# A transformer-like block in split fp32: the second product of an MLP unit accumulates in PSUM onto a ScalarE copy of the first

## The chip, the cores and the metric

The kernel runs on one core of a Trainium2 chip. The metric is the device time of one execution in microseconds (us). The core's engines run side by side, each through its own queue in order: TensorE (PE in the profile, with PEld for its weight loads), VectorE (DVE), ScalarE (ACT), GpSimd (POOL), and SyncE (SP), which here issues the DMAs. Matrix products land in PSUM, in banks of 128 x 512 fp32; everything else lives in SBUF.

## The reference

The input is 2048 tokens of width 576. After a layernorm two branches run on the same tokens, and their sum is added to the input:

```python
qkv = (x @ wqkv)                      # 32 heads of 18; each token looks at 8 keys, 2 apart, behind it
attn = softmax(logits, axis=-1)       # 8 logits per token and head
o = einsum("bhsw,bhswd->bhsd", attn, vg) ... @ wo

h = einsum("bsd,df->bsf", x, w1) + b1 # 576 -> 4608
act = h * tanh(softplus(h))           # mish
y = einsum("bsf,fd->bsd", act, w2)    # 4608 -> 576

return x + A(layernorm(x)) + B(layernorm(x))
```

## The kernel before

**Products.** Every fp32 product is made of three TensorE products of split operands: a number is kept as a high part (a rounded copy, written by ScalarE) and a low part (what is left, a subtraction on VectorE or GpSimd), and hi·hi, hi·lo and lo·hi are summed in PSUM. On top of that the larger products use schemes with seven block products in place of eight, which need sums of blocks as operands (the tiles S, t0, t1 on the way in; u and pw on the way out).

**Units.** The tokens are worked in two halves (hf = 0, 1) of 1024, each held transposed as X0 and X1 with 512 tokens each. The 4608 hidden columns are worked in 18 *units* (q) of 256. `m1_part` makes one unit in six parts. A part is a few matmuls of 128x512 (`prod`, L669, six of them; `rest`, L675, two more for the last 64 rows of the contraction) into one of three banks h1, h2, h3, which come from a pool of four. After a part ScalarE may save a bank in SBUF (`take`, L703), and `mish` finishes a block: VectorE adds a saved bank to the bank (L714), ScalarE applies Mish (L715), casts the high part (L720), and GpSimd subtracts to get the low part (L721). The parts before:

- part 0: h1 = X0·wa (6 matmuls), ScalarE saves it as c11, h2 = 6 + 2 matmuls of X0·wa, block (0,0) = mish(h2 + c11);
- part 1: h3 = the product with t1 (6);
- part 2: t0·S1 accumulates onto h1 (6), ScalarE saves it as c21;
- part 3: t0·S0 and a rest onto h1 (6 + 2), saved as c22, block (1,1) = mish(h3 + c22);
- part 4: 6 + 2 onto h3, block (1,0) = mish(h3 + c21);
- part 5: wc·S2 and a rest onto h1 (6 + 2), block (0,1) = mish(h1).

The weight tiles wa, wc, t0 and t1 are made on the chip in the first half (cast by ScalarE at L254, low part at L255) and are kept in DRAM; in the second half SyncE fetches them (L282).

**The second MLP product** runs in *pairs*, po, 128x288 each. In half 0 these are `m2_pair` (L767), summed into SBUF by VectorE (L771). In half 1 the first 8 units feed a second seven-product scheme: block sums on VectorE or GpSimd (`u_sum`, L801), high part (`u_high`, L807, ScalarE), low part (`u_low`, L813, VectorE or GpSimd by name), and `p_item` (L859) multiplies them, 24 matmuls an item ("N" in the code); the last ten units go through `m2_cols` (L880), summed by VectorE (L883). Their operands are the tiles u_k_qq: k is the item, qq the unit of a pair of units.

**Attention** is elementwise work. Per pair of units of heads GpSimd multiplies (pr, L533), VectorE reduces (L538), takes the softmax with an Exp on ScalarE (L552 to L564; L564 is the last scaling of the weights L), GpSimd multiplies with v (pv, L571), VectorE reduces into og (L577), transposes it, and SyncE sends it to DRAM. 9 such steps per pair; the list `cuts` says behind which items of the plan they run. At the end `o_split` (L907 to L939) prepares each tile of attention outputs and `wo_part` (L1063) multiplies it with wo.

**Order.** `plan` is a list of items: functions, background work, a cost. `quad()` writes the sequence of a unit's parts, of pairs ("N", "C") and others; `spot()` gives places in a unit for attention steps; tables such as `ds` (items ahead of its use at which a block's high and low parts are made) and `early` (attention steps in the second half) set the rest. The last loop writes out per item: work held over as `soon` (such as the Exp), background work, work held over from the item before (`pend`: the mish of a part), and the item's own matmuls. Every engine then runs its instructions in the order in which they were written.

## Time and profile before

| what | value |
| --- | --- |
| median of 3 runs | 1117.38 us (1114.83 to 1117.51) |
| profiled execution | 1114.25 us, of which the profile's span is 1112.5 us |
| granted TensorE clock over the profiled run | 1.0 |
| TensorE busy | 1101.6 us, 6550 matmuls |
| VectorE, GpSimd, ScalarE busy | 849.5, 790.8, 499.5 us |
| DMA | 271.60 MB, 244 GB/s on the mean |

Columns of the views quoted below: in the timeline a row is the start (us), the duration (us; of several instructions together where it ends in x2 or more), the engine, the line, the operation, output<-input, shapes, count, and in brackets the idle time of that engine in front of it with what ended it. In the view of waits a row is engine, output, line <- releasing engine, its output and line: total us, how often, longest. In the groups of one line it is ns min/median/max, first and last start. Among the DMA rows the last number is the median time from issue to landing (us). Matmuls are pipelined: a row's duration is longer than the distance to the next matmul, so distances are taken from start to start.

### The profile page before, as it was taken

To read this page: it belongs to the slowest core of one execution; us is meant where nothing else is said; L and a number is where in the kernel's file an instruction comes from. 1 tells how busy PE (TensorE), PEld (TensorE's weight loads), DVE (VectorE), ACT (ScalarE), POOL (GpSimd) and SP (SyncE) were. 2 spreads that over 40 slices of the span, in tenths; PEclk is the share of its full clock that TensorE was granted. 3 is DMA by queue.
4 is the path that set the end of the run, shared out by engine and by line. 5 is a ranking of instruction groups with operands and counts; after the bars stand their busy time and mean duration, and the time that the engine had idled before them with its cause. 6 is when DMAs were issued, how large, how long until landed. Compare 5 with 4: busy or idle time off the path is not lost.

```text
span 1112.5 us, 18203 instructions
## 1 busy us (share of the span) xinstructions
PE 1101.6 (99%) x6550; PEld 1015.2 (91%) x6550; DVE 849.5 (76%) x1367; ACT 499.5 (45%) x917; POOL 790.8 (71%) x639
## 2 busy tenths in 40 slices
PE   9999999999999999999999999999999999999998
PEld 8999899999999999999999889989989999999998
DVE  6369788888889888897656577786776677777786
ACT  5544655544454544555333354433433344343353
POOL 2479777766679688785788676666688976867532
PEclk9999999999999999999999999999999999999999
DMA  6899696868777758675597898565664657776574
GB/s 202 283 312 316 225 356 214 285 233 276 258 242 264 268 208 301 249 249 204 190 323 241 245 375 307 211 196 196 220 222 170 209 195 223 244 288 219 171 232 142
DMA packets 178270, 271.60 MB, mean 244 GB/s; under 512 B 53218, under 2 KB 120068, under 8 KB 178180
## 3 DMA queue, kind: packets, MB, share of 16 engines
q1 hardware_dynamic: 178180, 270.44, 71.6%
q8 instruction: 52, 0.85, 0.3%
q14 instruction: 38, 0.31, 0.1%
HBM read 160.39 MB, written 110.00 MB: 243 GB/s over the span
## 4 chain that ended last, share of the span: by engine, by line
PE 87%; POOL 6%; DVE 3%; issue 2%; ACT 1%; DMA 0%; SPq 0%; POOLq 0%; DVEq 0%; ACTq 0%
PE h L669 28%; PE po L767 21%; PE pq L348 9%; PE po L880 9%; PE po L859 6%; PE h L675 5%; PE o L1063 5%; PE z L446 3%; POOL pv L571 2%; POOL accP L868 1%; POOL pr L533 1%; POOL act L721 1%; POOL s L620 1%; DMA acc<-in_x 0%; PE ta L75 0%
## 5 line engine op out<-in xcount | busy, mean ns | idle before, releaser
L767 PEld LDWEIGHTS po<-w,act 128*128 128x128 f32 x1728 | 236.4, 188 | 6.0 <-POOL act L721 0.4
L767 PE MATMUL po<-w,act 128*128 128x288 f32 x1728 | 240.7, 295 | 0.1
L533 POOL TENSOR_TENSOR pr<-q,kv 128x576 f32<-128x576 f32 x128 | 196.9, 1563 | 8.5 <-DMA q<-q_d 5.0
L721 POOL TENSOR_TENSOR act<-c,act 128x512 fp32r<-128x512 f32 x81 | 107.3, 1325 | 128.6 <-ACT act L720 128.6
L571 POOL TENSOR_TENSOR pv<-L,kv 128x576 f32<-128x576 f32 x128 | 177.9, 1484 | 26.1 <-DVE L L564 21.2
L771 DVE TENSOR_TENSOR acc<-po,acc 128x288 f32<-128x288 f32 x288 | 119.4, 448 | 29.9 <-PE po L767 29.0
L348 PE MATMUL pq<-wq,xt 128*128 128x432 f32 x672 | 136.5, 361 | 1.0 <-ACT xt L81 1.0
L880 PEld LDWEIGHTS po<-w,act 128*128 128x128 f32 x960 | 130.9, 188 | 4.6 <-DVE accP L883 1.8
L880 PE MATMUL po<-w,act 128*128 128x288 f32 x960 | 133.5, 295 | 1.0 <-DVE accP L883 1.0
L348 PEld LDWEIGHTS pq<-wq,xt 128*128 128x128 f32 x672 | 125.0, 188 | 8.0 <-ACT xt L81 1.8
L715 ACT ACTIVATE c<-c,b1c 128x512 f32<-128x512 f32 x81 | 58.7, 725 | 140.7 <-DVE c L714 140.4
L669 PE MATMUL h<-xt,t 128*128 128x512 f32 x432 | 110.6, 391 | 0.5 <-DVE rt L714 0.3
L669 PE MATMUL h<-S,t 128*128 128x512 f32 x432 | 110.5, 391 | 0.0
L577 DVE TENSOR_REDUCE og<-pv 128x144 f32<-128x1152 f32 x64 | 86.0, 1345 | 25.7 <-POOL pv L571 25.6
L669 PE MATMUL h<-xt,wa 128*128 128x512 f32 x432 | 104.1, 390 | 0.0
L538 DVE TENSOR_REDUCE L<-pr 128x64 f32<-128x1152 f32 x64 | 85.8, 1341 | 23.8 <-POOL pr L533 23.7
L703 ACT COPY c<-h 128x512 f32<-128x512 f32 x81 | 47.4, 586 | 124.1 <-PE h L675 73.0
L859 PEld LDWEIGHTS po<-pw,u 128*128 128x128 f32 x672 | 92.2, 188 | 5.4 <-DVE u L813 2.1
L859 PE MATMUL po<-pw,u 128*128 128x288 f32 x672 | 94.3, 295 | 2.5 <-DVE u L813 1.6
L669 PEld LDWEIGHTS h<-xt,wa 128*128 128x128 f32 x432 | 80.9, 188 | 17.0
L669 PEld LDWEIGHTS h<-xt,t 128*128 128x128 f32 x432 | 79.0, 188 | 15.7 <-DVE rt L714 0.7
L883 DVE TENSOR_TENSOR accP<-po,accP 128x288 f32<-128x288 f32 x160 | 68.9, 452 | 29.8 <-PE po L880 28.2
(228 smaller groups left out, 1853.8 us busy)
## 6 DMA issues: line engine op xcount, KB each, us to landing
kv<-kv_d SPq DMA_DIRECT2D x64, 396.0 KB, 5.1
kept_t<-t SPq DMA_DIRECT2D x36, 512.0 KB, 4.8
t<-kept_t SPq DMA_DIRECT2D x36, 512.0 KB, 6.7
rw<-in_w SPq DMA_DIRECT2D x36, 320.0 KB, 4.4
kept_wa<-wa SPq DMA_DIRECT2D x18, 640.0 KB, 4.7
kept_w<-w SPq DMA_DIRECT2D x20, 576.0 KB, 4.1
wa<-kept_wa SPq DMA_DIRECT2D x18, 640.0 KB, 5.2
w<-kept_w SPq DMA_DIRECT2D x20, 576.0 KB, 4.1
```

Source lines behind the costliest of these rows:

```text
L348: nc.tensor.matmul(pq[:, 0:432], XT[:, xi, tok], wt[wi][:, hl, 0:432], start=i == 0, stop=i == len(seq) - 1)
L533: nc.gpsimd.tensor_tensor(out=pr[:, x:x + hh], in0=q[:, j0 + x:j0 + x + hh, None, :].to_broadcast([P, hh, W, CU]), in1=win(kt, 0, CU, j0 + ...
L538: nc.vector.tensor_reduce(L[:, k, j0:j0 + hj].rearrange("p j w h -> p (j w h)"), pr.rearrange("p j w (h d) -> p (j w h) d", h=2), axis=AX, ...
L571: nc.gpsimd.tensor_tensor(out=pr[:, x:x + hj].rearrange("p j d w -> p j w d"), in0=L[:, k, x:x + hj, :, h:h + 1].to_broadcast([P, hj, W, DH]),
L577: nc.vector.tensor_reduce(og[:, c0:c0 + DH, :].rearrange("p d j -> p j d"), pr, axis=AX, op=ALU.add)
L669: nc.tensor.matmul(ph, wt[:, wl, wk * P:(wk + 1) * P], X[:, xs, :], start=first and i == 0, stop=last and i == len(seq) - 1, skip_group_ch ...
L721: nc.gpsimd.tensor_tensor(out=a[:, 1, :], in0=t, in1=a[:, 0, :].bitcast(F32), op=ALU.subtract)
L767: nc.tensor.matmul(po, acts[hf, q, b, j][:, al, tok], done["w2", hf, 2 * q + j][:, wl, c * HC:(c + 1) * HC], start=i == 0, stop=i == 5)
L771: nc.vector.tensor_tensor(out=t, in0=po, in1=t, op=ALU.add)
L859: nc.tensor.matmul(po, units[e, k, qq][:, al, tok], w[:, qq, wl, :], start=i == 0, stop=i == 5)
L880: nc.tensor.matmul(po, acts[hf, q, b, j][:, al, tok], done["w2", hf, 2 * q + j][:, wl, c * HC:(c + 1) * HC], start=i == 0, stop=i == 5)
L883: nc.vector.tensor_tensor(out=t, in0=po, in1=t, op=ALU.add)
```

## The change

1. In the units q >= 2 of both halves (32 of 36), `take(c11)` is gone. ScalarE copies bank h1 into bank h2, from PSUM to PSUM (L740 in the changed file), the t1 product follows on TensorE, and then the 6 + 2 matmuls of h2 accumulate onto the copy (`start=False`). Block (0,0) is then mish(h2) directly, without VectorE's add. The units 0 and 1 keep c11.
2. All three banks are taken at part 0, in the order 2, 3, 1. h2's matmuls are now part of part 1 (or a part 7 of its own in the units 0 and in unit 1 of the second half).
3. In unit 0 of the second half the t1 product is cut in 3 + 3 matmuls, the second three (part 6) placed ahead of part 5. The sequences of the second half's units 1, 2 and 9 change as in the diff.
4. The low part of the first item's second block (u_0_1) is made one item earlier; the attention steps of units 1 to 3 of the second half move (`early`), 11 in all as before; in the items with a copy that carry no attention step, work held over as `soon` (the Exp) now stands behind the copy.
5. At the end, the `o_split` steps of the first output tile are written behind the matmuls of the items and partly an item later.

```diff
-    def prod(ph, wt, off, X, hi, lo, first, last):
+    def prod(ph, wt, off, X, hi, lo, first, last, some=range(6)):
...
         if part == 0:
-            prod(bank(hf, q, 1), wa, 0, X0, 0, 5, True, True)
-            take(hf, q, "c11")
-            prod(bank(hf, q, 2), wa, 2, X0, 2, 7, True, False)
-            rest(cur[2], wa, 4, X0, 4)
-            mish(hf, q, 0, 0, cur[2], cur["c11"])
+            for n in (2, 3, 1):
+                bank(hf, q, n)
+            prod(cur[1], wa, 0, X0, 0, 5, True, True)
+            if q > 1:
+                nc.scalar.copy(cur[2], cur[1])
+            else:
+                take(hf, q, "c11")
         elif part == 1:
-            prod(bank(hf, q, 3), t1, 0, X1, 0, 5, True, True)
+            half = (hf, q) == (1, 0)
+            prod(cur[3], t1, 0, X1, 0, 5, True, True, range(3) if half else range(6))
+        elif part == 6:
+            prod(cur[3], t1, 0, X1, 0, 5, True, True, range(3, 6))
...
+        if part == 7 or (part == 1 and q and (hf, q) != (1, 1)):
+            prod(cur[2], wa, 2, X0, 2, 7, q < 2, False)
+            rest(cur[2], wa, 4, X0, 4)
+            mish(hf, q, 0, 0, cur[2], None if q > 1 else cur["c11"])
...
+                elif part == 5:
+                    mi(hf, 0, 6)
                 mi(hf, 0, part)
+                if part == 0:
+                    mi(hf, 0, 7)
...
-                seq = ((0, (0,)), (2, (1, 2)), (1, (3, 4)), (3, (5, 6)), (4, (7, 8)), (5, (9,)))
+                seq = ((0, (0,)), (1, (1,)), (2, (2,)), (7, (3, 4)), (3, (5, 6)), (4, (7, 8)), (5, (9,)))
...
-                seq = (0, 1, "N", 2, "N", 3, "N", 4, "N", 5) if q > 2 else (0, 2, "N", 1, "N", 3, "N", 4, "N", 5)
+                seq = (0, 1, "N", 2, "N", 3, "N", 4, "N", 5)
...
+            if (e, k, qq) == (0, 0, 1):
+                ds = (-2, -1, -1)
...
-    early = {0: (8,), 1: (0, 2, 4, 6, 8), 2: (0, 3, 6), 3: (0, 3, 6), 4: (0, 4, 7), 5: (0, 3, 7), 6: (1, 4, 7),
+    early = {0: (8,), 1: (0, 2, 5, 7), 2: (1, 5, 9), 3: (0, 2, 4, 7), 4: (0, 4, 7), 5: (0, 3, 7), 6: (1, 4, 7),
...
-        before(j + (1, 1, 2, 3)[k], lambda k=k: o_split(0, k, True))
+        plan[j + (1, 2, 2, 3)[k]][0].append(lambda k=k: o_split(0, k, True))
...
+    seeded = {at["m", hf, q, 0] for hf in range(NH) for q in range(2, NP)}
...
-        for fn in first + bg + (fns + held if i == at["m", 0, 1, 0] else held + fns):
+        if i in seeded and i not in cuts[0] + cuts[1]:
+            order = bg + held + fns + first
+        else:
+            order = first + bg + (fns + held if i == at["m", 0, 1, 0] else held + fns)
```

The changed lines stand one lower from L664 on and ten to eleven lower from `m2_pair` on. Three places show how instructions move.

*A unit in the steady part of the first half (unit 6).* TensorE's queue before (h_0_6 are banks of unit 6, the number behind tells them apart; wa, t its weights; xt the tokens):

```order
L669 MATMUL h_0_6_2801<-xt_0_227,wa_6_2538 128x512 x6
L669 MATMUL h_0_6_2810<-xt_0_227,wa_6_2538 128x512 x6
L675 MATMUL h_0_6_2810<-xt_0_227,wa_6_2538 128x512 x2
L669 MATMUL h_0_6_2829<-xt_1_511,t_0_6_2709 128x512 x6
L767 MATMUL po_5_1_0_0_2844<-w_0_10_2505,act_1_10_2741 128x288 x3
```

And in the changed kernel:

```order
L670 MATMUL h_0_6_2799<-xt_0_227,wa_6_2527 128x512 x6
L670 MATMUL h_0_6_2798<-xt_1_511,t_0_6_2705 128x512 x6
L670 MATMUL h_0_6_2797<-xt_0_227,wa_6_2527 128x512 x6
L676 MATMUL h_0_6_2797<-xt_0_227,wa_6_2527 128x512 x2
L777 MATMUL po_5_1_0_0_2839<-w_0_10_2502,act_1_10_2737 128x288 x3
```

The t1 product has moved ahead of the eight matmuls of h2, which makes room for the copy. ScalarE's queue at the same place, before:

```order
L703 COPY c_0_6_2808<-h_0_6_2801 128x512
L254 CAST wa_7_2822<-rw_14_2713 128x640
L715 ACTIVATE c_0_6_2808<-c_0_6_2808,b1c 128x512
L720 CAST act_0_12_2826<-c_0_6_2808 128x512
L254 CAST w_0_13_2836<-rw_13_2711 128x576
```

And now:

```order
L740 COPY h_0_6_2797<-h_0_6_2799 128x512
L254 CAST wa_7_2810<-rw_14_2709 128x640
L254 CAST w_0_13_2827<-rw_13_2707 128x576
L716 ACTIVATE mn_0_12_2826<-h_0_6_2797,b1c 128x512
L721 CAST act_0_12_2836<-mn_0_12_2826 128x512
```

The saving copy is now a copy from bank to bank, and Mish reads the bank.

*The start of unit 2 of the second half, where the first item N multiplies u_0_0 and u_0_1.* VectorE before, from the softmax of attention pair 0 (m_0, L_0) to the low part of u_0_1:

```order
L552 TENSOR_REDUCE m_0_7408<-L_0_7318 128x32
L554 TENSOR_TENSOR L_0_7318<-L_0_7318,m_0_7408 128x256
L714 TENSOR_TENSOR rt_7265<-h_1_1_7397,rt_7265 128x512
L562 TENSOR_REDUCE m_0_7408<-L_0_7318 128x32
L563 RECIPROCAL m_0_7408<-m_0_7408 128x32
L564 TENSOR_TENSOR L_0_7318<-L_0_7318,m_0_7408 128x256
L714 TENSOR_TENSOR rm_7262<-h_1_1_7397,rm_7262 128x512
L801 TENSOR_TENSOR rm_7262<-ra_7256,rm_7262 128x512
L577 TENSOR_REDUCE og_0_7441<-pv_0_0_0_7442 128x8x18
L801 TENSOR_TENSOR rm_7261<-rt_7264,rm_7261 128x512
L714 TENSOR_TENSOR ra_7257<-h_1_2_7499,ra_7257 128x512
L813 TENSOR_TENSOR u_0_1_7510<-rm_7262,u_0_1_7510 128x512
```

And now:

```order
L552 TENSOR_REDUCE m_0_7418<-L_0_7302 128x32
L554 TENSOR_TENSOR L_0_7302<-L_0_7302,m_0_7418 128x256
L715 TENSOR_TENSOR rm_7240<-h_1_1_7342,rm_7240 128x512
L811 TENSOR_TENSOR rm_7240<-ra_7234,rm_7240 128x512
L823 TENSOR_TENSOR u_0_1_7468<-rm_7240,u_0_1_7468 128x512
L811 TENSOR_TENSOR rm_7239<-rt_7242,rm_7239 128x512
L562 TENSOR_REDUCE m_0_7418<-L_0_7302 128x32
L563 RECIPROCAL m_0_7418<-m_0_7418 128x32
L564 TENSOR_TENSOR L_0_7302<-L_0_7302,m_0_7418 128x256
```

The low part has moved ahead of the normalisation of L_0 and of the reduce of pv_0_0_0, and the add from h_1_2 is gone. On GpSimd, before:

```order
L813 TENSOR_TENSOR u_0_0_7421<-rm_7261,u_0_0_7421 128x512
L571 TENSOR_TENSOR pv_0_0_0_7442<-L_0_7318,kv_1_0_7322 128x4x8x18 x2
L571 TENSOR_TENSOR pv_0_0_1_7483<-L_0_7318,kv_1_0_7322 128x4x8x18 x2
L813 TENSOR_TENSOR u_1_0_7470<-rt_7264,u_1_0_7470 128x512
L813 TENSOR_TENSOR u_1_1_7527<-rt_7265,u_1_1_7527 128x512
```

And now:

```order
L823 TENSOR_TENSOR u_0_0_7400<-rm_7239,u_0_0_7400 128x512
L571 TENSOR_TENSOR pv_0_0_0_7477<-L_0_7302,kv_1_0_7306 128x4x8x18 x2
L823 TENSOR_TENSOR u_1_0_7443<-rt_7242,u_1_0_7443 128x512
L823 TENSOR_TENSOR u_1_1_7501<-rt_7243,u_1_1_7501 128x512
L823 TENSOR_TENSOR u_2_0_7540<-ra_7233,u_2_0_7540 128x512
```

One product pv_0_0 fewer stands ahead of the low parts of item 1 (u_1_0, u_1_1), and what stands there reads an L_0 that is normalised later than u_0_1's low part.

*The last pairs ahead of the first output tile.* VectorE before, from the last reduce of the last attention pair (og_7):

```order
L577 TENSOR_REDUCE og_7_11482<-pv_7_1_1_11628 128x8x18
L914 TENSOR_TENSOR s_0_11680<-ot_0_11676,o_1_11589 128x256
L917 TENSOR_TENSOR ob_11674<-ot_0_11676,ob_11674 128x256
L929 TENSOR_TENSOR s_0_11687<-s_0_11680,ot_0_11677 128x256
L930 TENSOR_TENSOR s_0_11687<-ot_0_11677,o_1_11589 128x256
L883 TENSOR_TENSOR accP_1_7475<-po_17_1_1_0_0_11695,accP_1_7475 128x288
L883 TENSOR_TENSOR accP_1_7475<-po_17_1_1_0_1_11703,accP_1_7475 128x288
L883 TENSOR_TENSOR accP_1_7477<-po_17_1_1_1_0_11711,accP_1_7477 128x288
L883 TENSOR_TENSOR accP_1_7477<-po_17_1_1_1_1_11719,accP_1_7477 128x288
```

And now:

```order
L577 TENSOR_REDUCE og_7_11450<-pv_7_1_1_11596 128x8x18
L893 TENSOR_TENSOR accP_1_7448<-po_17_1_1_0_0_11643,accP_1_7448 128x288
L893 TENSOR_TENSOR accP_1_7448<-po_17_1_1_0_1_11651,accP_1_7448 128x288
L893 TENSOR_TENSOR accP_1_7450<-po_17_1_1_1_0_11659,accP_1_7450 128x288
L893 TENSOR_TENSOR accP_1_7450<-po_17_1_1_1_1_11667,accP_1_7450 128x288
L924 TENSOR_TENSOR s_0_11682<-ot_0_11678,o_1_11557 128x256
L927 TENSOR_TENSOR ob_11676<-ot_0_11678,ob_11676 128x256
L593 STREAM_TRANSPOSE oT_7_11686<-og_7_11450 128x576
L893 TENSOR_TENSOR accP_0_7445<-po_17_0_0_0_0_11688,accP_0_7445 128x288
```

The sums of the pairs po_17_1_1 have moved ahead of the output tile's preparation (s_0, ob), and two operations of that preparation have moved behind the next four sums.

More of the change, by code (lines that the diff above doesn't have):

```diff
@@ L664, in bank @@
         return cur[n]
-    def prod(ph, wt, off, X, hi, lo, first, last):
+    def prod(ph, wt, off, X, hi, lo, first, last, some=range(6)):
         seq = [(off + k, wl, xs + k) for k in range(2) for wl, xs in ((0, hi), (0, lo), (1, hi))]
-        for i, (wk, wl, xs) in enumerate(seq):
+        for i in some:
+            wk, wl, xs = seq[i]
             nc.tensor.matmul(ph, wt[:, wl, wk * P:(wk + 1) * P], X[:, xs, :],
@@ L752, in m1_part @@
             mish(hf, q, 1, 0, cur[3], cur["c21"])
-        else:
+        elif part == 5:
             prod(cur[1], wc, 0, Ss[hf, 2], 0, 2, False, False)
@@ L1144, in block_kernel @@
     US = {"q": 2.75, "z": 2.5, "p": 3.15, "t": 0.6, "o": 2.6}
-    PART = (3.2, 1.4, 1.4, 1.8, 1.8, 1.8)
+    PART = (1.4, 3.2, 1.4, 1.8, 1.8, 1.8, 0.7, 1.8)
     def add(tag, *fns, alias=None):
@@ L1236, in quad @@
                     qi(hf, NQ - 1, 0, JB - 1)
+                elif part == 5:
+                    mi(hf, 0, 6)
                 mi(hf, 0, part)
+                if part == 0:
+                    mi(hf, 0, 7)
                 for i in ids:
@@ L1248, in quad @@
             elif q == 2 * OC + 1:
-                seq = (("N", (0,)), (0, ()), ("N", (1,)), (1, ()), (2, (2,)), ("C", (3,)), (3, (4,)), ("C", (5,)), (4, (6,)), ("C", (7,)), (5, (8,)), ("C", (9,)))
+                seq = (("N", (0,)), (0, ()), (1, ()), ("N", (1,)), (2, (2,)), ("C", (3,)), (3, (4,)), ("C", (5,)), (4, (6,)), ("C", (7,)), (5, (8,)), ("C", (9,)))
             elif q % 2 == 0:
-                seq = (0, 1, "N", 2, "N", 3, "N", 4, "N", 5) if q > 2 else (0, 2, "N", 1, "N", 3, "N", 4, "N", 5)
+                seq = (0, 1, "N", 2, "N", 3, "N", 4, "N", 5)
                 seq = [(p_, (i,)) for i, p_ in enumerate(seq)]
@@ L1546, in block_kernel @@
         held, pend[:] = pend[:], []
-        for fn in first + bg + (fns + held if i == at["m", 0, 1, 0] else held + fns):
+        if i in seeded and i not in cuts[0] + cuts[1]:
+            order = bg + held + fns + first
+        else:
+            order = first + bg + (fns + held if i == at["m", 0, 1, 0] else held + fns)
+        for fn in order:
             fn()
```

## The prediction

> **What bounds the kernel now.** I read the page first (busy times, granted clock, chain that ended last), then what TensorE waits for, then the timeline around each place where it stops.

> ```profile
> PE 1101.6 (99%) x6550; PEld 1015.2 (91%) x6550; DVE 849.5 (76%) x1367; ACT 499.5 (45%) x917; POOL 790.8 (71%) x639
> PEclk9999999999999999999999999999999999999999
> PE 87%; POOL 6%; DVE 3%; issue 2%; ACT 1%; DMA 0%; SPq 0%; POOLq 0%; DVEq 0%; ACTq 0%
> ```

> TensorE is busy for 1101.6 of 1112.5 us at full clock in all slices, and the chain is 87% TensorE. The change leaves the 6550 matmuls and their shapes alone, so it can win only from the 10.9 us in which TensorE idles. This is where that idle time goes:

> ```profile
> PE po L859 <- DVE u L813: 1.6, 1, 1.6
> PE po L880 <- DVE accP L883: 1.0, 1, 1.0
> PE po L859 <- ACT u L807: 0.8, 1, 0.8
> PE h L669 <- ACT rt L703: 0.7, 1, 0.7
> PE h L669 <- DVE rt L714: 0.3, 1, 0.3
> PE h L669 <- DVE c L714: 0.2, 1, 0.2
> ```

> Each of these is one event, so the forecast is a sum over places and not a rate per unit. The removed VectorE add is not a cost of its own in most units: a steady unit runs without a gap.

> ```profile
> 356.18 2.88 PE L669 MATMUL h<-xt,wa 128*128 128x512 f32 x12
> 358.89 0.62 PE L675 MATMUL h<-xt,wa 128*128 128x512 f32 x2
> 359.35 1.52 PE L669 MATMUL h<-xt,t 128*128 128x512 f32 x6
> 357.74 0.59 ACT L703 COPY c<-h 128x512 f32<-128x512 f32 x1
> ```

> Twelve matmuls take 358.89 - 356.18 = 2.71 us from start to start, so a 128x512 one takes 0.226. (24 po matmuls of 128x288 take 3.18 us, 0.1325 each, by the same reading.)

> **The copy (32 units).** h1's six matmuls end their issue at 356.18 + 1.36 = 357.54, and the copy begins 0.2 us later. In the new order the t1 product fills 357.54 to 358.90; the copy must have landed by then. At 0.59 us it ends at 358.33: 0.57 us to spare, so the 32 new waits cost nothing while the copy takes under 0.59 + 0.57 = 1.16 us, less some 0.05 for the signal. No row of before copies from PSUM to PSUM. The nearest are these:

> ```profile
> L925 ACT COPY ot<-o x8: 578/582/584, 1042.4 to 1097.3; 128x512 f32<-128x512 f32 x8
> L714 DVE TENSOR_TENSOR c<-h,c x81: 652/682/693, 111.2 to 1033.4; 128x512 f32<-128x512 f32 x81
> ```

> SBUF to PSUM is 0.58 us, PSUM to SBUF 0.59. The low bound is 0.58; the high one, if each side were paid in full, 1.17, which would make each unit wait about 0.06 us, 32 x 0.06 = 2 us. I take 0.6, since both rows stream 512 elements at the same price, whichever side is in PSUM: 0 us. [...]

> The copy is late only where ScalarE is backed up. Unit 15 of the first half is one:

> ```profile
> 452.64 2.88 PE L669 MATMUL h<-xt,wa 128*128 128x512 f32 x12
> 455.32 0.58 ACT L703 COPY c<-h 128x512 f32<-128x512 f32 x1
> ```

> The t1 product would end at 452.64 + 2.71 = 455.35 and the copy at 455.90: +0.6 us with the signal. What backs ScalarE up there is an Exp, which waits for VectorE, and VectorE loses one 0.68 us add a unit (32 x 0.68 = 22 us of its 849.5). Bounds 0 and +0.7; I take **+0.4**. Where an Exp stood directly ahead of the copy, the order now puts it behind; behind the copy on ScalarE wait only casts of the next weights, as before.

> **Unit 0 of the second half, the copy c22.**

> ```profile
> 632.19 0.63 PE L675 MATMUL h<-xt,wc 128*128 128x512 f32 x2
> 632.86 0.58 ACT L703 COPY rt<-h 128x512 f32<-128x512 f32 x1 [2.56 <-PE h L675]
> 633.49 1.66 PE L669 MATMUL h<-S,wc 128*128 128x512 f32 x6 [0.68 <-ACT rt L703]
> ```

> From 632.19 + 2 x 0.226 = 632.64 to 633.49 TensorE stands 0.85 us for the copy. Three matmuls of t1 (0.68 us) now stand there: 0.17 is left, **-0.7**. They are taken from part 1, where h1's c21 copy has other work beside it.

> **Unit 2 of the second half: t1 is needed earlier, u_0_1 is ready earlier.** In all units t1 is now needed 8 x 0.226 = 1.8 us earlier; in this unit, where a part 2 stood ahead of it too, 8 + 6 matmuls and a whole item N earlier.

> ```profile
> 650.34 2.88 PE L669 MATMUL h<-xt,wa 128*128 128x512 f32 x12
> 644.75 0.32 SPq L282 DMA_DIRECT2D t<-kept_t  x1
> t<-kept_t SPq DMA_DIRECT2D x2, 512.0 KB, 8.2
> t<-kept_t SPq DMA_DIRECT2D x36, 512.0 KB, 6.7
> ```

> t1's first matmul would come at 650.34 + 1.36 = 651.70. Its fetch is issued at 644.75, when the last matmul that reads its buffer is done, so both move up together by the 0.7 above. At the median landing of all 36 fetches (6.7) it lands at 651.45: no wait. At the one that the DMA rows of 639 to 652 us show (8.2) it lands at 652.95: +1.25. I take **+0.5**.

> Then the first item N:

> ```profile
> 651.19 1.55 DVE L801 TENSOR_TENSOR rm<-ra,rm 128x512 f32<-128x512 f32 x1 [0.91 <-ACT rm L715]
> 653.93 1.61 DVE L801 TENSOR_TENSOR rm<-rt,rm 128x512 f32<-128x512 f32 x1
> 655.46 0.68 DVE L714 TENSOR_TENSOR ra<-h,ra 128x512 f32<-128x512 f32 x1
> 656.06 1.16 DVE L813 TENSOR_TENSOR u<-rm,u 128x512 fp32r<-128x512 f32 x1
> 654.88 0.82 PE L859 MATMUL po<-pw,u 128*128 128x288 f32 x5
> 657.27 2.78 PE L859 MATMUL po<-pw,u 128*128 128x288 f32 x19 [1.57 <-DVE u L813]
> ```

> VectorE makes the low part of u_0_1 behind an og reduce, a sum and an add; TensorE stands from 654.88 + 5 x 0.1325 = 655.54 to 657.27, 1.73 us. The low part now follows the sum of 651.19 and ScalarE's cast: about 650.5 + 1.55 + 0.6 + 1.16 = 653.8, ahead of the need at about 655.3. **-1.7.**

> What is late next is item 2's left operand. Its low parts are GpSimd's:

> ```profile
> 657.96 1.30 POOL L813 TENSOR_TENSOR u<-rt,u 128x512 fp32r<-128x512 f32 x1 [1.30 <-ACT u L807]
> 659.22 2.52 POOL L571 TENSOR_TENSOR pv<-L,kv 128x576 f32<-128x576 f32 x2
> ```

> In the new order a pv pair (2.52) stands ahead of them, and L_0 is normalised on VectorE only behind u_0_1 and one more sum: about 653.8 + 1.6 + 0.9 = 656.3. So pv ends at 658.8, the low parts at 660.1 and 661.4. Item N begins near 654.7, lasts 3.18, six matmuls of part 2 follow (1.36): item 2 needs the first low part at 659.5 and the second at 659.9. +1.5 if all of this holds, 0 if VectorE's sums run near the add's 0.68. I take **+0.7**. The other attention steps that move (11 before, 11 after), with their loads of q and kv and stores of o_d on SyncE's queue, lie beside items with no wait in before: 0, bounds -0.3 and +0.3. Most loads on that queue keep their order.

> **VectorE's adds on the path.** Elsewhere an add of c11, or what queues with it, ended a wait:

> ```profile
> 747.12 0.65 DVE L813 TENSOR_TENSOR u<-rm,u 128x512 fp32r<-128x512 f32 x1
> 746.91 2.37 PE L859 MATMUL po<-pw,u 128*128 128x288 f32 x14
> 864.80 0.68 DVE L714 TENSOR_TENSOR c<-h,c 128x512 f32<-128x512 f32 x1
> 121.01 1.63 PEld L767 LDWEIGHTS po<-w,act 128*128 128x128 f32 x12 [0.37 <-POOL act L721]
> ```

> At 747 the 14 matmuls should take 14 x 0.1325 + 0.16 = 2.02 us and take 2.37: they wait 0.35 for u, whose queue loses an add of 0.68. At 781 the wait for rt L714 (0.3 in the list, 0.45 with the restart, which at 633 was 0.17) loses one too. Both go. At 865 the wait is for the c22 add (0.2, 0.4 with the restart), which queues behind a reduce of attention; the Exp ahead of that now comes earlier, since no add of c11 stands ahead of it: it goes too. At 121 the cast of t1 has moved ahead of unit 1's activations on ScalarE: 0.4, gone. Together **-1.6**, bounds -1.6 and -0.4 (747 alone, which is the surest). The 0.8 behind ACT u L807 stays.

> **The first output tile.**

> ```profile
> 1048.05 0.42 DVE L930 TENSOR_TENSOR s<-ot,o 128x256 f32<-128x256 f32 x1
> 1048.38 1.54 DVE L883 TENSOR_TENSOR accP<-po,accP 128x288 f32<-128x288 f32 x4
> 1045.72 2.15 PE L880 MATMUL po<-w,act 128*128 128x288 f32 x15
> 1048.88 2.38 PE L880 MATMUL po<-w,act 128*128 128x288 f32 x16 [1.01 <-DVE accP L883]
> ```

> The four sums that free po's banks come behind four operations of the tile (4 x 0.33 from start to start). TensorE stands from 1045.72 + 15 x 0.1325 = 1047.71 to 1048.88: 1.17. Ahead of the four, the sums come 1.3 us earlier: **-1.1**. The preparation that moves back is read by the tile's own matmuls later; what it may cost there is 0 to 0.3, I take **+0.1**.

> **Sum.** -0.7 - 1.7 - 1.6 - 1.1 + 0.4 + 0.5 + 0.7 + 0.1 = -3.4 us against the profiled 1114.25. The median is 3.1 us above that execution; taken off the median it gives **1114.0 us** (-0.30%). All gains and no loss would be -5.1; all losses in full and the small gains at their lower bounds: -0.7 - 1.7 - 0.4 - 1.1 + 0.7 + 1.25 + 1.5 + 0.3 = -0.2.

> **Rivals.**
> (a) *The gains are eaten in the second half's first units*: t1 lands late and GpSimd's low parts come behind pv, both in full (+0.75 and +0.8 over what I took). For: DMA and GpSimd rows above; against: VectorE is relieved there. -1.8 us: 1115.5.
> (b) *All gains, no loss*: for: each stall is one event with a named cause that the order removes; against: the chain of attention moves too. -5.1 us: 1112.3.
> (c) *Slower: the copy is on the path.* TensorE now waits for ScalarE within 1.36 us, 32 times, where before it had 3.2 us. To turn -3.4 into +3.4 it takes 6.8 / 32 = 0.21 us a unit, which is a copy of some 1.35 us, or ScalarE as late as in unit 15 in a third of the units. For: no row prices the copy, and in before unit 15 is late already; against: both sides at 0.58, and the 0.57 us to spare in a steady unit. 1121.
> (d) *VectorE's relief speeds GpSimd*, which would shorten low parts and attention. The sums of L801 take 1.55 to 1.61 us above and GpSimd works beside them, while the adds of L714 keep to 652 to 693 ns over 81 runs: the adds don't contend, so taking them away relieves nothing there. 0 us. [...]

> **Chances.** Forecast (-2 to -5 us) 0.50, (a) 0.22, (b) 0.15, (c) 0.13. About 0.3% (3.4 us) is what a measurement of this kernel can tell from no change. Faster by more than that: 0.30 of the forecast's 0.50 and all of (b), 0.45; within: 0.20, 0.22 of (a) and 0.01 of (c), 0.43; slower 0.12. The range leaves out most of (c) and the far end of (b): 1109.5 to 1118.5.

> **What would show it.** In the profile after: TensorE's waits lose the rows for u L813 (1.6), accP (1.0) and rt L703 (0.7), and its idle time falls from 10.9 to about 7.5 us; ScalarE's copies h<-h take some 0.6 us, 32 of them, and no matmul of h waits for them but in unit 15. The forecast is wrong if a row "h <- ACT h" adds up to over 2 us, if the low parts of the second item or the fetch of t1 hold TensorE for more than 2 us together, or if VectorE's relief shows up nowhere on TensorE.

## The result and the profile after

The changed kernel is slower: 1124.5 us median (1121.82 to 1126.71, 5 runs) against 1116.9 us of the kernel before (5 runs), a ratio of 1.0073 with a 95% interval of 1.0051 to 1.0094. Measured again on another occasion it was 1121.83 against 1114.38 us, 1.0067 (1.0052 to 1.0082). The prediction was 1114.0 us, range 1109.5 to 1118.5. Both the sign and the size were wrong.

The first profile after is one of 1126.44 us, with a span of 1124.7 us, 12.2 us longer than before. Its busy times and its chain of work that ended last:

```profile
PE 1107.4 (98%) x6550; PEld 1019.2 (91%) x6550; DVE 834.3 (74%) x1335; ACT 499.0 (44%) x917; POOL 792.1 (70%) x639
PE 90%; DVE 4%; POOL 3%; ACT 1%; DMA 1%; issue 1%; SPq 0%; ACTq 0%; DVEq 0%; POOLq 0%
```

VectorE lost 15 us of work, as meant (1367 to 1335 instructions). The same 6550 matmuls took 5.8 us longer, and TensorE's idle time rose from 10.9 to 17.3 us. The view of TensorE's waits says at whom it stood:

```profile
PE po L890 <- DVE accP L893: 3.9, 1, 3.9
PE h L670 <- DMA t<-kept_t: 2.7, 1, 2.7
PE po L869 <- ACT u L817: 2.4, 1, 2.4
...
PE h L670 <- DVE rt L715: 1.0, 1, 1.0
...
PE h L670 <- DVE c L715: 0.7, 1, 0.7
PE h L670 <- ACT h L740: 0.4, 1, 0.4
```

The rows that the prediction wanted gone are gone: the 1.6 behind u L813 and the 1.0 behind accP at the first output tile, the 0.7 behind rt L703. In their place stand three waits of 2.4 to 3.9 us, single events again, at 655.9, 822.8 and 846.1 us. They cost more than they last. The busy time by stretches of 20 us, with the granted TensorE clock behind the brackets:

```profile
640.00:660.00 20.00, 17.34 (x70) 13.93 (x69) 10.56 (x16) 10.78 (x18) 7.20 (x6) 0.91 1.00 341
820.00:840.00 20.00, 17.53 (x101) 16.03 (x100) 11.74 (x19) 5.18 (x9) 12.72 (x9) 0.91 0.50 156
840.00:860.00 20.00, 16.15 (x92) 14.79 (x92) 9.85 (x18) 3.98 (x6) 19.53 (x16) 0.91 0.27 94
```

The columns are the stretch and its length, then PE, PEld, DVE, ACT and POOL with their instruction counts, the clock, the DMA share and GB/s. The clock is 1.0 in the whole profile before, and 0.91 in these three stretches: for 3.4 us each, from 655.96, 823.21 and 847.11 us, the granted clock is 0.5. There a 128x512 matmul takes 0.427 us from start to start in place of 0.227, and a 128x288 one 0.240 in place of 0.133. From start to start the waits are 2.8, 2.6 and 4.0 us, and the slow matmuls behind them add 1.7, 1.6 and 1.6.

The moments of these changes of the clock show when they come. In every profile they lie a whole number of 3.41 us apart (here 1, 49, 50, 56 and 57 times behind the first), so each run can be cut into stretches of 3.41 us, and the waits end at different places in them (here 0.07, 0.4 and 1.0 us ahead of an edge). In the 16 profiles of this document (from 20 us on, the very end left out) TensorE was busy, by the profile's rows, for at most 1.65 us in 17 such stretches at full clock, and each was followed by one at half clock; in all the others at full clock, some 5000, it was busy for 1.68 us or more, and none was. In the profile after, the three were busy for 0.75, 1.00 and 1.00 us; in the one before, at full clock throughout, none was busy for less than 1.92 us. Each half clock lasted to the end of the first stretch in which TensorE was busy throughout: one to four stretches. So in these runs the half clock followed where a wait left TensorE idle for 1.76 us or more of one stretch (3.41 - 1.65), and not where it left 1.73 us or less.

The copy itself does what the prediction said. Its group of all 32, and a steady unit (12) with ScalarE's copy:

```profile
L740 ACT COPY h<-h x32: 570/570/583, 141.4 to 1031.5; 128x512 f32<-128x512 f32 x32
```

```profile
381.36 1.52 PE L670 MATMUL h<-xt,wa 128*128 128x512 f32 x6
382.72 1.53 PE L670 MATMUL h<-xt,t 128*128 128x512 f32 x6
384.09 1.08 PE L670 MATMUL h<-xt,wa 128*128 128x512 f32 x4
383.23 0.58 ACT L740 COPY h<-h 128x512 f32<-128x512 f32 x1
```

The copy takes 0.57 us and ends at 383.81, 0.28 us ahead of h2's first matmul, though it began late here. From one unit's first matmul to the next one's it is alternately 24.15 and 24.08 us, before and after.

### The profile page after: what moved, and what is told of

Its sections match the earlier page's. It is cut to its first block, busy times and chain, and to the rows that moved or that the text cites. A ratio compares the mean times of both kernels' runs of the same rounds, so it can differ in the third digit from the quotient of the medians.

```text
span 1124.7 us, 18106 instructions
## 1 busy us (share of the span) xinstructions
PE 1107.4 (98%) x6550; PEld 1019.2 (91%) x6550; DVE 834.3 (74%) x1335; ACT 499.0 (44%) x917; POOL 792.1 (70%) x639
## 4 chain that ended last, share of the span: by engine, by line
PE 90%; DVE 4%; POOL 3%; ACT 1%; DMA 1%; issue 1%; SPq 0%; ACTq 0%; DVEq 0%; POOLq 0%
PE h L670 29%; PE po L777 20%; PE po L890 11%; PE pq L348 9%; PE po L869 7%; PE h L676 5%; PE o L1073 4%; PE z L446 3%; POOL pv L571 1%; DMA t<-kept_t 1%; POOL s L620 1%; DVE u L823 1%; DMA acc<-in_x 0%; PE ta L75 0%; POOL pr L533 0%
## 5 line engine op out<-in xcount | busy, mean ns | idle before, releaser
L571 POOL TENSOR_TENSOR pv<-L,kv 128x576 f32<-128x576 f32 x128 | 178.9, 1493 | 35.3 <-DVE L L564 18.8
L722 POOL TENSOR_TENSOR act<-c,act 128x512 fp32r<-128x512 f32 x56 | 73.6, 1315 | 127.9 <-ACT act L721 124.3
L781 DVE TENSOR_TENSOR acc<-po,acc 128x288 f32<-128x288 f32 x288 | 122.1, 451 | 44.7 <-PE po L777 43.6
L670 PE MATMUL h<-xt,wa 128*128 128x512 f32 x432 | 110.3, 391 | 0.4 <-ACT h L740 0.4
L704 ACT COPY c<-h 128x512 f32<-128x512 f32 x56 | 32.8, 587 | 132.1 <-PE h L676 77.4
L670 PEld LDWEIGHTS h<-S,t 128*128 128x128 f32 x432 | 77.7, 188 | 13.2 <-ACT rm L704 0.5
## 6 DMA issues: line engine op xcount, KB each, us to landing
kept_t<-t SPq DMA_DIRECT2D x36, 512.0 KB, 4.6
t<-kept_t SPq DMA_DIRECT2D x36, 512.0 KB, 5.8
```

The source lines that it names most:

```text
L571: nc.gpsimd.tensor_tensor(out=pr[:, x:x + hj].rearrange("p j d w -> p j w d"), in0=L[:, k, x:x + hj, :, h:h + 1].to_broadcast([P, hj, W, DH]),
L670: nc.tensor.matmul(ph, wt[:, wl, wk * P:(wk + 1) * P], X[:, xs, :], start=first and i == 0, stop=last and i == len(seq) - 1, skip_group_ch ...
L722: nc.gpsimd.tensor_tensor(out=a[:, 1, :], in0=t, in1=a[:, 0, :].bitcast(F32), op=ALU.subtract)
L781: nc.vector.tensor_tensor(out=t, in0=po, in1=t, op=ALU.add)
```

## The experiments

My theory after the two profiles: the copy is free, and the loss is a few long stalls, each with a cause of its own in what was moved along with the copy, and each lengthened by a slower clock. The rivals: the copy costs after all; the stalls are accidents of a run; a mended stall only moves on.

**The changed kernel once more.**

> The changed kernel once more, unchanged, for a second profile. If the three long stalls of the first profile (t1's fetch in unit 2 of the second half 2.8 us, the item at 822.8 us 2.6 us, the pair at 846 us 4.0 us) come from the order of the instructions, all three stand here again within 0.5 us, and the granted clock drops behind each. If the one at 822.8, where one VectorE subtraction took 4.47 us in place of 1.64, is an accident of arbitration between VectorE and GpSimd, it is shorter here by 1 us or more. If the t1 fetch was slow by accident of the DMA, its stall is between 0.5 and 1.5 us here.

Measured: 1121.83 us. The stalls from start to start: 2.06 us ahead of t1 with no slow matmuls behind it, 1.76 at 694 us, 0.98 at 819.7, and 4.04 at 841.4 with 1.6 us of slow matmuls. So the last one belongs to the order, the first varies, and the one at 822.8 was an accident in its length. VectorE's subtraction ahead of it, in the first profile of the changed kernel and what GpSimd did beside it:

```profile
816.02 4.47 DVE L823 TENSOR_TENSOR u<-ra_r,u 128x512 fp32r<-128x512 f32 x1 [0.20 <-ACT u L817]
815.81 1.36 POOL L811 TENSOR_TENSOR ra<-ra,rm 128x512 f32<-128x512 f32 x1
817.05 2.89 POOL L533 TENSOR_TENSOR pr<-q,kv 128x576 f32<-128x576 f32 x2
```

And in the second:

```profile
814.45 1.64 DVE L823 TENSOR_TENSOR u<-ra_r,u 128x512 fp32r<-128x512 f32 x1 [0.20 <-ACT u L817]
814.23 1.31 POOL L811 TENSOR_TENSOR ra<-ra,rm 128x512 f32<-128x512 f32 x1
815.47 3.74 POOL L533 TENSOR_TENSOR pr<-q,kv 128x576 f32<-128x576 f32 x2
```

In both the subtraction starts 0.2 us behind a GpSimd instruction. In the second it is done at 816.1, 0.6 us into GpSimd's next instructions, which are then slower (3.74 us in place of 2.89); in the first it lasts past all three of GpSimd's (to 819.9) and is done 0.5 us behind. In the profile before, VectorE's low parts took 0.64 to 0.69 us at the seven places where GpSimd ran nothing beside them. Here, beside GpSimd, it is 1.64 and 4.47 us; the order is the same in both and the outcome is not, and no run shows why.

**Unit 9's sequence as before.**

```diff
-                seq = (("N", (0,)), (0, ()), (1, ()), ("N", (1,)), (2, (2,)), ...
+                seq = (("N", (0,)), (0, ()), ("N", (1,)), (1, ()), (2, (2,)), ...
```

> The changed kernel with the sequence of the second half's unit 9 as before (N, part 0, N, part 1). Theory: the 4.0 us stall at 846 us comes from this, because the attention step tied to that N slid behind three splits and two joins on GpSimd and VectorE's reduce of it stands ahead of the sums that free po's banks; then the stall goes, with its half clock (1.6 us): 5 to 6 us faster than the changed kernel, about 1119. Rival, that it comes from VectorE and GpSimd being late anyway behind the stall at 822.8: less than 1.5 us faster.

Measured: 1117.62 us, 4.2 us less than the changed kernel in the same session; the stall of 4 us is gone. GpSimd and VectorE in the first profile of the changed kernel show how it came about, with TensorE's row last:

```profile
837.51 2.82 POOL L878 TENSOR_TENSOR accP<-accP,accP 128x576 f32<-128x576 f32 x2
840.28 1.29 POOL L832 TENSOR_TENSOR act<-rm,act 128x512 fp32r<-128x512 f32 x1
841.53 2.78 POOL L533 TENSOR_TENSOR pr<-q,kv 128x576 f32<-128x576 f32 x2
844.34 1.35 DVE L538 TENSOR_REDUCE L<-pr 128x64 f32<-128x1152 f32 x1 [8.32 <-POOL pr L533]
845.61 1.54 DVE L893 TENSOR_TENSOR accP<-po,accP 128x288 f32<-128x288 f32 x4
846.11 3.17 PE L890 MATMUL po<-w,act 128*128 128x288 f32 x15 [3.85 <-DVE accP L893]
```

VectorE sat idle for 8.32 us at a reduce that needs GpSimd's product pr, and behind the reduce stand the four sums that free po's banks. With the sequence as before, pr stands ahead of one join (accP) and one split (act) that it stands behind in the changed kernel; at 2.8 and 1.3 us they take as long as the stall:

```profile
833.40 2.81 POOL L533 TENSOR_TENSOR pr<-q,kv 128x576 f32<-128x576 f32 x2
836.17 2.83 POOL L878 TENSOR_TENSOR accP<-accP,accP 128x576 f32<-128x576 f32 x2
838.95 1.30 POOL L832 TENSOR_TENSOR act<-rm,act 128x512 fp32r<-128x512 f32 x1
838.24 3.34 PE L890 MATMUL po<-w,act 128*128 128x288 f32 x24
```

**pw_2's fetch behind t0 and t1 of unit 2.**

```diff
-        before(lead + 1, lambda e=e, k=k: p_fetch(e, k))
+        before(lead + 1 + 6 * (g == 2), lambda e=e, k=k: p_fetch(e, k))
```

> The changed kernel with the fetch of pw_2 (576 KB, needed some 15 us later) taken from ahead of unit 2's t0 and t1 to behind them. Theory: t1's fetch queues behind other transfers, and one transfer less brings it 1.7 to 2.6 us earlier: the stall of 2.8 us falls under 1.2 us, no drop of the clock follows it, and the kernel is 3 to 4 us faster than the changed one, about 1121. Rival, that the fetch is slow by itself or waits for its buffer: no change of that stall, same time as the changed kernel.

Measured: 1122.08 us, no gain, though the stall is gone. In the changed kernel, first profile, SyncE's queue and TensorE:

```profile
643.85 0.60 SPq L837 DMA_DIRECT2D pw<-kept_B  x1
644.50 1.94 SPq L282 DMA_DIRECT2D t<-kept_t  x2
655.89 2.84 PE L670 MATMUL h<-xt,t 128*128 128x512 f32 x6 [2.66 <-DMA t<-kept_t]
```

And with pw_2 moved:

```profile
642.77 3.60 SPq L282 DMA_DIRECT2D t<-kept_t  x2
649.94 1.30 SPq L837 DMA_DIRECT2D pw<-kept_B  x1
653.00 1.53 PE L670 MATMUL h<-xt,t 128*128 128x512 f32 x6
661.68 0.67 PE L869 MATMUL po<-pw,u 128*128 128x288 f32 x3 [0.25 <-POOL u L823]
662.91 1.36 PE L869 MATMUL po<-pw,u 128*128 128x288 f32 x8 [0.56 <-POOL u L823]
```

t1 comes in time, and the wait that the prediction put at item 2, behind GpSimd's low parts, turns up: 0.4 and 0.7 us from start to start. Under the long stall it had been covered. Of the 2.06 us that the repeated profile shows, 1.1 come back here, and 0.7 more by the clock: behind the 4.0 us wait of unit 9, which stands in this kernel too, it is halved for two stretches (838.5 to 845.3) in place of one.

**The copy alone, on the kernel before.** Only parts 0 and 1 of the units from 2 on are rewritten, and unit 2 of the second half takes the even units' order:

```diff
+        elif part == 0:
+            for n in (2, 3, 1):
+                bank(hf, q, n)
+            prod(cur[1], wa, 0, X0, 0, 5, True, True)
+            nc.scalar.copy(cur[2], cur[1])
```

> The kernel before with the copy alone: in units 2 to 17 of both halves h1 is copied from bank to bank, t1's product stands between h1 and h2, the add of c11 is gone; unit 2 of the second half takes the order of the other even units, since its own would leave nothing beside the copy. No other slot moves. If the copy costs nothing (theory), every steady unit is without a wait and the kernel is within 3 us of the kernel before but for waits at unit 2 of the second half (t1's fetch, u_0_1): 1114 to 1121. If the copy itself is what makes the changed kernel slower, all or most of the 7.6 us stand here: 1123 to 1126.

Measured: 1122.99 us, 1.0077 (1.0062 to 1.0092). The rival's number, but not by its mechanism: the wait for the copy is three events.

```profile
PE h L669 <- ACT h L744: 6.1, 3, 3.4
```

They are 3.6 us at 193 us with 2.7 of slow matmuls behind, 0.6 at 462, and 2.4 at 907. At the first and the third, ScalarE held the copy behind an Exp that waited for VectorE (2.0 and 2.9 us). In the changed kernel the Exp stands behind the copy at both, and TensorE waits at neither; that edit was not tried alone. And the 0.84 us (c22), 1.67 (t1) and 1.14 (output tile) of this run show the places that the other edits of the change were for.

**The attention steps of units 1 to 3 as before, on top of unit 9's sequence.**

```diff
-    early = {0: (8,), 1: (0, 2, 5, 7), 2: (1, 5, 9), 3: (0, 2, 4, 7), ...
+    early = {0: (8,), 1: (0, 2, 4, 6, 8), 2: (0, 3, 6), 3: (0, 3, 6), ...
```

> The changed kernel with the sequence of unit 9 as before and the attention steps of the second half's units 1 to 3 as before. Theory: the stall at 694 us (0.8 to 1.8 us, waiting for the add of L714 in unit 3) comes from the fourth attention step in unit 3, whose reduce and GpSimd multiplications stretch VectorE's subtraction from 0.67 to 1.85 us; it goes, and the kernel is 1 to 2 us faster than with the sequence of unit 9 alone, if the fetch of t1 in unit 2 stays as late as it was (2 to 2.8 us); some 1116. If the moved steps are also what made that fetch late, it falls under 1 us, and the kernel is at 1113 to 1114. Rival, that the steps don't matter: 1117 to 1118.

Measured: 1113.76 us, 0.9994 (0.9985 to 1.0003): as fast as the kernel before. Unit 9's sequence and the attention steps account for all of the 7.5 us that the changed kernel lost. In the changed kernel's second profile VectorE at unit 3 ran beside a product of GpSimd's fourth step (first row):

```profile
689.43 2.82 POOL L533 TENSOR_TENSOR pr<-q,kv 128x576 f32<-128x576 f32 x2
690.96 1.85 DVE L823 TENSOR_TENSOR u<-rm,u 128x512 fp32r<-128x512 f32 x1
693.33 0.68 DVE L715 TENSOR_TENSOR rt<-h,rt 128x512 f32<-128x512 f32 x1
694.07 1.67 PE L670 MATMUL h<-xt,t 128*128 128x512 f32 x6 [1.60 <-DVE rt L715]
```

With the steps as before:

```profile
688.09 0.67 DVE L823 TENSOR_TENSOR u<-rm,u 128x512 fp32r<-128x512 f32 x1
689.29 0.67 DVE L715 TENSOR_TENSOR rt<-h,rt 128x512 f32<-128x512 f32 x1
```

TensorE no longer waits there. The stall ahead of t1 fell to 1.04 us, but in part only by moving: 1.24 us now stand in unit 1, at 648.3 us, ahead of it.

**All three, and the copy first in units 9 and 15 of the first half.**

> As the run before, and with pw_2's fetch behind unit 2's t0 and t1, and with h1's product and the copy written ahead of the held-over work of the first half's units 9 and 15, so that the copy doesn't queue behind two casts and Mish. Theory: the stalls left in the changed kernel are single events with single causes, so the t1 stall (2 us or more) and the two late copies (0.16 and 0.6 us) go: 2 to 4 us below the run before, 1111 to 1114, at or below the kernel before. Rival, that each mended stall turns up again a few us later: within 1 us of the run before.

Measured: 1114.67 us, 1.0000 (0.9991 to 1.0009), 0.9 more than the run before: the rival's number. t1's stall is gone, 0.7 and 0.5 us stand behind it instead at 670 and 672 us, and 0.8 at 129.7; the 1.24 in unit 1 stay. The late copies were still there (0.16 and 0.6 us): both items carry an attention step and so take the other branch of the loop, which the edit did not touch.

**The copy first, with the edit in the right branch.**

```diff
+            if i in (at["m", 0, 9, 0], at["m", 0, 15, 0]):
+                order = fns + first + bg + held
```

> The changed kernel with unit 9's sequence and the attention steps of units 1 to 3 as before (1113.8), and in the first half's units 9 and 15 the product of h1 and the copy written ahead of everything held over, which the edit of the earlier run did not reach, because these two items carry an attention step. Theory: the copy is late there only because Mish and two to three casts stand ahead of it on ScalarE; both waits (0.3 and 0.8 us with the restart) go: 1 us faster, 1112.8. Rival, that what is pushed back (the casts, Mish of block (0,1)) is waited for instead: 1113.8 or more.

Measured: 1113.03 us, 0.9991 (0.9982 to 0.9999). Both waits are gone, as the theory had it.

**Unit 1's steps as changed, unit 3's as before.** On top of the run above, `early = {1: (0, 2, 5, 7), 2: (0, 3, 6, 9), 3: (0, 3, 6)}`.

> As the run beside it, but with unit 1's attention steps as in the change (four, at 0, 2, 5, 7), the fifth put at the end of unit 2 (0, 3, 6, 9), and unit 3 with three as before. Theory: unit 1's 1.24 us wait (for the c22 add, at 648 us) comes from the steps at 4, 6 and 8 and goes, unit 3's doesn't come back; 1 to 2 us faster than the run beside it, 1111 to 1112. Rival: the step at the end of unit 2 makes unit 3 or t1's fetch late again: 1113 to 1116.

Measured: 1115.29 us, 1.0011 (0.9997 to 1.0024). The 1.24 us in unit 1 and the stall in unit 3 are both gone, and t1's stall is back: 2.64 us, and 1.6 us of slow matmuls. The rival's number. With nothing to hold TensorE in unit 1, it reaches the need for t1 1.3 us sooner behind the issue of the fetch than in the run above, and the fetch takes 9.5 us from issue to landing in place of 8.4.

**The same, with pw_2's fetch behind t0 and t1.**

> g2_steps (1115.3) with pw_2's fetch behind unit 2's t0 and t1. Theory: t1's fetch lands late because of the transfers ahead of it, so its stall of 2.6 us and the 1.6 us of half clock behind it go, of which some 1.1 us come back at item 2, whose low parts on GpSimd stand behind a pv pair: 1112 to 1113, below the kernel before. Rival, that the stall only moves on to the items behind it: 1115 to 1116.

Measured: 1112.56 us, 0.9987 (0.9978 to 0.9996). t1's stall falls from 2.64 to 1.34 us, the slow matmuls are gone, and only 0.3 us come back (at 690.7). The fetch now takes 8.2 us. The mended stall does not move on here. This is the lowest median of all, 0.13% below the kernel before, though its interval overlaps that of the run with the copy first; what is left on TensorE are single waits of 0.2 to 1.3 us.

**The change without the copy**, on the kernel with unit 9's sequence and the steps as before:

```diff
-            if q > 1:
-                nc.scalar.copy(cur[2], cur[1])
-            else:
-                take(hf, q, "c11")
+            take(hf, q, "c11")
```

> The changed kernel with unit 9's sequence and the attention steps as before (1113.8), but without the copy: ScalarE saves c11 in SBUF in all units, h2 starts anew, and VectorE adds, as in the kernel before; all else stays as in the change. Theory: the copy takes nothing and gives only the few waits behind L714; these (at 747, 781 and 865 us, 1.2 us together) come back, the late copies of units 9 and 15 (1.0 us) no longer hold TensorE: within 1 us of 1113.8. Rival, that relieving VectorE of 32 adds is worth more, because attention runs ahead: 1116 or more.

Measured: 1114.04 us, 0.9998 (0.9990 to 1.0007), against 0.9994 with the copy. The waits change places (0.45 us at 462.8, 0.95 at 662.7 and 0.29 at 739 come; the late copies go), and the sum is the same within what was measured. h2's matmuls start anew here, and VectorE's add is back. So within about 1 us the copy is neither the loss nor a gain.

**The attention step of unit 9 in its old slot, the sequence as changed.**

```diff
-                seq = (("N", (0,)), (0, ()), (1, ()), ("N", (1,)), (2, (2,)), ...
+                seq = (("N", (0,)), (0, ()), (1, (1,)), ("N", ()), (2, (2,)), ...
```

with the steps of units 1 to 3 as before.

> The changed kernel with the attention steps of units 1 to 3 as before and unit 9's sequence as in the change (N, 0, 1, N), but with the second attention step of unit 9 at part 1, the slot in which it stood before, and not at the N behind it. Theory: not the sequence but the step's slot makes the 4 us stall, since GpSimd's multiplication for it falls behind three splits and two joins; then the stall is gone here too: 1113 to 1115. Rival, that the sequence itself does it (part 1 ahead of N): some 1118.

Measured: 1114.16 us, 0.9998 (0.9989 to 1.0007). No stall at 846. The slot of one attention step, and not the order of TensorE's parts, made the 4 us. (The steps of units 1 to 3 went back too; they stand 150 us ahead of the stall, and no run has the slot alone put back.)

**The copy twice**, on the kernel with unit 9's sequence as before (a second `nc.scalar.copy(cur[2], cur[1])`).

> The changed kernel with the sequence of unit 9 as before, and with the copy from bank to bank done twice in all 32 units (0.48 us more each). If the copy lies beside t1's product with 0.55 us to spare (theory), most units still don't wait: 0 to 4 us slower than with the sequence of unit 9 alone (1117.6). If the copy is on the path (rival), 32 x 0.48 = 15 us slower.

Measured: 1125.92 us, 8.3 us more, between the two. A steady unit, ScalarE's two copies and TensorE:

```profile
214.30 0.57 ACT L740 COPY h<-h 128x512 f32<-128x512 f32 x1
214.90 0.57 ACT L741 COPY h<-h 128x512 f32<-128x512 f32 x1
215.52 1.65 PE L670 MATMUL h<-xt,wa 128*128 128x512 f32 x6
```

The second copy ends at 215.47, and h2 starts 0.06 us late. Each steady unit grew by 0.22 us (24.37 and 24.29), which over 32 units is 7 of the 8.3: 0.06 us of wait and 0.16 of a slower restart (0.11 of it on the next matmul). In four units the second copy came later still (0.4 to 1.2 us of wait). So one copy has about 0.5 us to spare, and here even a wait of 0.06 us had a price of 0.16 us on top.

**Stalls of chosen length**, on the kernel before: c11 is copied over and over in some units of the first half, which holds TensorE ahead of part 2.

```diff
+        if hf == 0 and name == "c11":
+            for _ in range({4: 14, 6: 16, 8: 17, 10: 18, 12: 20, 14: 24, 16: 32}.get(q, 0)):
+                nc.scalar.copy(t, cur[1])
```

> The kernel before with its c11 copy repeated 14, 16, 17, 18, 20, 24 and 32 times in the first half's units 4, 6, 8, 10, 12, 14 and 16, which only makes TensorE wait ahead of part 2. Estimated stalls, from 0.48 us a copy against 6.4 us of cover: 1.3, 2.3, 2.8, 3.2, 4.2, 6.1 and 10 us. Theory: a stall over some 2.5 us is followed by matmuls at half rate for 3 to 4 us, one of up to 2.3 us is not. Then units 4 and 6 go on at 0.227 us a 128x512 matmul, and units 10 to 16 at 0.43 for 3 to 4 us. Rival, that the slow stretches belong to the places where they were seen: full rate behind all seven.

Measured: 1184.6 us (one run). The stalls came out longer than estimated, 4.4 to 14.3 us, and slow matmuls for 3.4 to 5.8 us followed all seven. It says nothing on shorter ones, so a second run had 11 to 13 copies more in units 6 to 16.

> The kernel before with c11 copied 12, 13, 12, 11, 12 and 11 times more in the first half's units 6, 8, 10, 12, 14 and 16; estimated stalls from the earlier run with repeats (4.38 us at 16 copies in unit 6, 4.99 at 17 in unit 8, 5.94 at 18 in unit 10, 7.14 at 20, 9.31 at 24, about 0.57 us a copy): 2.0 to 2.7 us. Theory: TensorE goes on at full rate behind a stall of up to 2.4 us and at half rate for 3 to 4 us behind one of 2.5 or more, whatever made the stall. Rival, that length alone doesn't decide: both outcomes on both sides of 2.45 us.

Measured: 1131.37 us (one run), the stalls from start to start 1.92, 2.54, 2.26, 1.61, 1.92 and 1.36 us. The rival: length alone does not decide. TensorE's rows behind the first and the second, and the windows of 4 us at the first, second and third:

```profile
244.86 2.46 PE L669 MATMUL h<-S,t 128*128 128x512 f32 x6 [1.76 <-ACT c L706]
297.41 1.66 PE L669 MATMUL h<-S,t 128*128 128x512 f32 x6 [2.38 <-ACT c L706]
```

```profile
245.00:249.00 4.00, 4.00 (x14) 3.23 (x15) 4.00 (x9) 3.77 (x7) 1.98 (x2) 0.57 0.46 168
297.00:301.00 4.00, 3.03 (x16) 2.42 (x17) 3.61 (x8) 3.84 (x8) 1.43 (x2) 1.00 0.35 132
349.00:353.00 4.00, 3.29 (x19) 2.67 (x20) 4.00 (x8) 3.20 (x6) 1.98 (x2) 1.00 0.00 0
```

Behind the first wait of 1.92 us the clock was halved, behind 2.54 and 2.26 and the second 1.92 it was not. The stretches of 3.41 us, counted from the change of the clock at 245.44 us, show the difference:

| wait | stretch | TensorE busy in it (us) | clock in the next |
| --- | --- | --- | --- |
| 1.92, the first | 242.02 to 245.44 | 1.65 | 0.5 |
| 2.54 | 293.22 to 296.64 | 1.81 | 1.0 |
| 2.54 | 296.64 to 300.05 | 2.08 | 1.0 |
| 2.26 | 344.43 to 347.84 | 2.33 | 1.0 |
| 2.26 | 347.84 to 351.25 | 1.68 | 1.0 |
| 1.92, the second | 446.82 to 450.24 | 2.03 | 1.0 |

The first wait lies in one stretch; the others are cut in two by the edge between stretches.

## Why the prediction was wrong

By its own steps:

- *The copy, 0 us*: right. 0.57 us each, steady units unchanged, and with the copy undone the time is the same.
- *The copy late in unit 15, +0.4*: undersized. It cost 0.6 and 0.1 us of restart there and 0.27 in unit 9; VectorE's relief did not bring the Exp forward (it waits 1.75 us for VectorE in both kernels). Written first, the copy no longer holds TensorE in either.
- *Unit 0's c22 copy, -0.7*: right in kind, smaller: 0.95 us became 0.20 + 0.14 with restarts of 0.1 each, -0.4.
- *The first item N, -1.7*: right, the wait for u_0_1 is gone. *Item 2's low parts, +0.7*: 1.1 us where t1 comes in time; hidden behind t1's stall in the changed kernel.
- *VectorE's adds on the path, -1.6*: the four waits are gone, but 0.9 us with the restart came at 129.7, behind VectorE's add in unit 1 of the first half; -0.7.
- *The first output tile, -1.1 + 0.1*: the wait is gone; the preparation that moved back costs 0.7 at the tile's own matmuls (1068 and 1083 us), not 0.1.
- *t1's fetch in unit 2, +0.5, bounds 0 and +1.25*: mis-sized, 2.1 to 2.8 us, and 1.7 more by the clock in the first profile. The need comes 6.95 us behind the issue, as forecast; what was wrong is the length of the fetch. The 8.2 us of the bound are those of t0's fetch before; t1's own took 7.5 us there, 9.6 and 8.9 in the two profiles of the changed kernel, where pw_2's fetch has moved from between t0's and t1's to ahead of both, and 6.7 where pw_2's stands behind both.
- *"The other attention steps that move ... lie beside items with no wait in before: 0, bounds -0.3 and +0.3."* This is the step that failed. A place without a wait in the trace of before says that its slack was not used up; it says nothing of how large the slack is. The steps in units 1 to 3 cost 3.9 us together (unit 9's sequence apart): 0.8 to 1.8 in unit 3, and most of the rest at t1, which they let TensorE reach 1.3 us earlier behind the issue of the same fetch.
- *Unit 9's sequence* had no term at all: a term put at nothing without a reason. The step tied to the moved N slid behind one more join and one more split on GpSimd; 4.0 us and 1.6 of half clock, 4.2 us by the medians. I had read this on TensorE's queue, where it is a swap of two parts, and not on GpSimd's, where the order shows it.
- *A stall costs its length*, as the whole sum takes it: wrong where a stall left TensorE busy for no more than 1.65 us of a 3.41 us stretch. That is 4.9 us (1.7 + 1.6 + 1.6) of the 12.2 in the first profile.

The run with unit 9's sequence and the steps as before came out at -0.5 us in place of -3.4: the gains and losses above, without t1's fetch and item 2, come to some -2.2, and in that run 1.0 us at t1 and 1.2 in unit 1 take up most of it (the 1.2 go with unit 1's changed steps). Rival (a) had the right place, the second half's first units, and a price of 1.6 us in place of 4 to 6 (t1, unit 3 and the half clock); rival (c), which held the chance of slower, had the wrong mechanism.

What stays open: why t1's fetch takes 7.5 us in the profile before, 9.6 in the first after and 8.2 in the fastest version, beyond the one transfer whose place was tried; how the step tables act on it apart from TensorE's own pace; and why VectorE's subtraction ahead of 822.8 us took 4.47 us in one run and 1.64 in another with the same order.

## What to carry to other kernels

When work is moved, read the new order on every in-order engine that the moved item touches, not on the bottleneck alone: a reduce that waited 8.32 us for GpSimd held everything behind it on VectorE, and two swapped items cost 4 us because one small step hung on one of them. A place without a wait is not a place with room; measure its slack (a doubled instruction does that) before calling a move free. And a stall can cost more than its length: in these runs one that left TensorE busy for 1.65 us or less of one 3.41 us stretch cost the half clock behind it too, 1.6 to 2.7 us. Length alone does not tell which: of two waits of 1.92 us in one run, the half clock followed one and not the other.
